# Reordering the first tile's attention, its first row blocks, the next tile's k copies and the last rows of a fused attention and MLP kernel

## The chip, the cores and the metric

One core of a Trainium2 chip. The metric is the device time of one execution in microseconds (us), median of several. Executions of one and the same kernel scatter here by about 2 us, which is as large as the effects looked for. So I read segments of profiles beside times, and give 95% intervals with every ratio.

## The reference

Chunked attention (chunks of 64 tokens, head size 64), then an MLP with exact Gelu:

```python
q, k, v: (8, 8, 576, 64) float32
scores = q_c @ k_c^T / 8;  attn = softmax(scores);  x = attn @ v_c      # per chunk of 64
h = x @ w_in (512 x 2048);  g = 0.5 * h * (1 + erf(h / sqrt(2)));  out = g @ w_out (2048 x 512)
```

The kernel cuts the 4608 tokens into nine tiles of 512. For each tile TensorE makes q k^T, the AV products (x), then `mm1` (h) and `mm2` (y); the attention of the next tile is woven into the present tile's mm2.

## The kernel before

The parts that the change and the argument touch; "..." marks cuts. An "AV" is the group of matmuls that makes x for one head pair; a "spread" is sixteen small matmuls that copy the reciprocals of the softmax sums to where x needs them; a "cast" turns a loaded float32 piece into bfloat16.

```python
DV, AC, PO = nc.vector.tensor_copy, nc.scalar.copy, nc.gpsimd.tensor_copy

def att_Tk(t, g, copy):                       # k of head pair g, transposed into two diagonal halves
    tp = transposed(t, "k", g)                # four 128x128 transposes into one PSUM bank
    for r in range(2):
        sl = slice(CH * r, CH * (r + 1))
        copy(k_bds[g][sl, :, sl].rearrange(...), tp[sl])
...
T += [lambda g=g: att_Tq(t, g, cq), lambda g=g: att_Tk(t, g, ck if t == 0 or g < 2 else DV)]
...
def att_total(t, g0, g1):                     # tiles 2 to 8: the softmax sums, on VectorE
    ...
    nc.vector.tensor_tensor(total[:, g0:g1], part[:, g0:g1], other[:, g0:g1], op=add)
    nc.vector.reciprocal(rb[:, g0:g1], total[:, g0:g1])
...
def mm1_slot(t, f, n=1, between={}):          # n blocks of h at a time, step by step over ks
    ...
    for ks in range(KS):
        for a in range(n):
            nc.tensor.matmul(h_ps[a][:], w_in_sb[:, ks, ...], st["x"][:, ks, :], ...)
    for a in range(n):
        nc.scalar.activation(st["h"][:, f + a, :], h_ps[a][:], Act.Gelu)
...
def last_rows(t, ms):                         # the last 128 rows: two groups of 256 columns
    h = d_model // 2
    for a, (pool, tag) in enumerate(((ps_mm, "mm"), (ps_at, "at"))):
        y_ps = pool.tile([P, h], f32, ...)
        for f in range(FF):
            nc.tensor.matmul(y_ps[:], ...[P rows of h], w_out_sb[:, f, a * h:(a + 1) * h], ...)
        y_sb = ypool.tile([P, h], f32, ...)
        (AC if a == 0 else DV)(y_sb[:], y_ps[:])
        for c in range(P // CH):
            (nc.sync if c == 0 else nc.scalar).dma_start(out[..., a * h:(a + 1) * h], y_sb[...])

def mm2_rows(t, f):                           # tile 0's mm2: block f of w_out for four row blocks
    for ms in range(MT // P):
        if f == 0:
            pool, tag = (ps_at, "at") if ms == 3 else (ps_mm, "mm")
            tiles[t]["y_ps", ms] = pool.tile(...)
        nc.tensor.matmul(tiles[t]["y_ps", ms][:], ..., start=(f == 0), stop=False)
...
A[0](); p2(); A[1](); p3(); A[2](); keep_warm(1); A[3]()     # AVs; p2, p3 spread the sums
win.append(load_w_in(NWC - 1)); wout = [load_w_out(0)]
for i, eng in enumerate((PO, AC, DV, PO)):                   # casts of the first w_in chunk
    win[0](i, eng)
act_table(Act.Gelu)
```

The loads are issued in one order: tile 0's q, k, v, then w_in, then w_out, q, k and v of tile 1 in between.

The softmax here doesn't subtract the row's maximum and nothing guards it: scores larger than these inputs give would overflow.

Of the kernel before, what the change touches and what calls it, by code (L numbers as in the profile page):

```python
# [11 lines left out]
def kernel(  # L12
# [9 lines left out]
    nc = tc.nc  # L22
    P = 128
    f32 = mybir.dt.float32
    bf16 = mybir.dt.bfloat16
    Act = mybir.ActivationFunctionType

    B, H, S, D = q.shape
    CH = 64
    NC = S // CH  # L30
    J = 4
    PC = CH // J
    G = H // 2
    d_model = H * D
# [3 lines left out]
    MT = CT * CH  # L38
    NT = B + 1
    KS = d_model // P  # L40
    FF = d_ff // P
# [27 lines left out]
    k_bds = [consts.tile([P, CT, P], bf16, name=f"k_bd{i}") for i in range(G)]  # L69
# [10 lines left out]
    w_out_sb = consts.tile([P, FF, d_model], bf16, name="w_out_sb")  # L80
# [10 lines left out]
    ypool = ctx.enter_context(tc.tile_pool(name="ypool", bufs=4))  # L91
    ps_mm = ctx.enter_context(tc.tile_pool(name="ps_mm", bufs=3, space=bass.MemoryType.PSUM))
    ps_tp = ctx.enter_context(tc.tile_pool(name="ps_tp", bufs=2, space=bass.MemoryType.PSUM))
    ps_at = ctx.enter_context(tc.tile_pool(name="ps_at", bufs=3, space=bass.MemoryType.PSUM))
# [6 lines left out]
    tiles = [dict() for _ in range(NT)]  # L101
# [38 lines left out]
    def transposed(t, nm, g):  # L140
        pool, tag = (ps_tp, "tp") if t or nm == "q" else (ps_mm, "mm")
        tp = pool.tile([P, 2, J, P], bf16, tag=tag, name="tp")
        for j in range(J):
            nc.tensor.transpose(tp[:, 0, j], tiles[t][nm][:, g, j].rearrange("p r d -> p (r d)"), ident[:])  # L144
        return tp[:, 0].rearrange("p j (i c) -> p i c j", i=CT)

    def att_Tq(t, g, copy):
        tp = transposed(t, "q", g)
        qT = work.tile([P, CT, CH], bf16, tag="qT", name="qT", bufs=5)
        copy(qT[:].rearrange("p i (c j) -> p i c j", j=J), tp)  # L150
        tiles[t]["qT", g] = qT

    def att_Tk(t, g, copy):
        tp = transposed(t, "k", g)
        for r in range(2):
            sl = slice(CH * r, CH * (r + 1))
            copy(k_bds[g][sl, :, sl].rearrange("p i (c j) -> p i c j", j=J), tp[sl])  # L157


    def flip(t, nm):  # L160
# [7 lines left out]
    def flip_k(t, g, copy):  # L168
        src = flipped(t, "k", g)
        for r in range(2):  # L170
            sl = slice(CH * r, CH * (r + 1))
            copy(k_bds[g][sl, :, sl].rearrange("p i (c j) -> p i c j", j=J), src[sl])  # L172

    def att_S_flipped(t, g):

        st = tiles[t]
        s_ps = ps_at.tile([P, CT, CH], f32, tag="at", name="s_ps")
        qt = st["qt"][:, g * J:(g + 1) * J].rearrange("p j (i c) -> p i j c", i=CT)
        for i in range(CT):
            nc.tensor.matmul(s_ps[:, i, :].rearrange("p (j c) -> p j c", j=J), k_bds[g][:, i, :], qt[:, i],  # L180
                             start=True, stop=True)
        pT = work.tile([P, CT, CH], bf16, tag="pT", name="pT", bufs=5)
        nc.scalar.activation(pT[:].rearrange("p i (c j) -> p i c j", j=J),  # L183
                             s_ps[:].rearrange("p i (j c) -> p i c j", j=J), Act.Exp, scale=scale)
        st["pT", g] = pT

    def att_S(t, g):
        st = tiles[t]
        pool, tag = (ps_tp, "tp") if t == 1 and g > 1 else (ps_at, "at")
        s_ps = pool.tile([P, CT, CH], f32, tag=tag, name="s_ps")  # L190
        for i in range(CT):
            nc.tensor.matmul(s_ps[:, i, :], k_bds[g][:, i, :], st["qT", g][:, i], start=True, stop=True)  # L192
        pT = work.tile([P, CT, CH], bf16, tag="pT", name="pT", bufs=5)
        nc.scalar.activation(pT[:], s_ps[:], Act.Exp, scale=scale)  # L194
        st["pT", g] = pT
# [49 lines left out]
    def att_total(t, g0, g1):  # L245

        part, other, total, rb = (tiles[t][nm] for nm in ("part", "other", "total", "rb"))
        for s in range(G):
            o = s ^ 1
            nc.scalar.copy(other[QD * s:QD * (s + 1), g0:g1], part[QD * o:QD * (o + 1), g0:g1])  # L250
        nc.vector.tensor_tensor(total[:, g0:g1], part[:, g0:g1], other[:, g0:g1], op=mybir.AluOpType.add)
        nc.vector.reciprocal(rb[:, g0:g1], total[:, g0:g1])
# [46 lines left out]
    DV, AC, PO = nc.vector.tensor_copy, nc.scalar.copy, nc.gpsimd.tensor_copy  # L299

    def att_units(t, cq=DV, ck=DV):
        tiles[t]["x"] = xpool.tile([P, G, MT], bf16, tag="x", name="x")
        T = []
        for g in range(G):
            T += [lambda g=g: att_Tq(t, g, cq), lambda g=g: att_Tk(t, g, ck if t == 0 or g < 2 else DV)]
        S_ = [lambda g=g: att_S(t, g) for g in range(G)]
        if t > 1:
            T = [lambda g=g: flip_k(t, g, ck) for g in range(G)]
            S_ = [lambda g=g: (att_S_flipped(t, g), att_part(t, g)) for g in range(G)]
        if t > 0:  # L310
            U = [lambda g=g: att_total(t, g, g + 2) for g in (0, 2)] + [lambda g=g: att_rc(t, g) for g in range(G)]
        else:
            U = [lambda g=g: att_sum(t, g) for g in range(G)]
        A = [lambda g=g: att_av(t, g) for g in range(G)]
        return T, S_, U, A
# [46 lines left out]
                nc.sync.dma_start(out[m0:m0 + CH, :], y_sb[c * CH:(c + 1) * CH, :])  # L362

    def last_rows(t, ms):
        h = d_model // 2
        for a, (pool, tag) in enumerate(((ps_mm, "mm"), (ps_at, "at"))):
            y_ps = pool.tile([P, h], f32, tag=tag, name="y_ps")
            for f in range(FF):
                nc.tensor.matmul(y_ps[:], tiles[t]["h"][:, f, ms * P:(ms + 1) * P],  # L369
                                 w_out_sb[:, f, a * h:(a + 1) * h], start=(f == 0), stop=(f == FF - 1))  # L370
            y_sb = ypool.tile([P, h], f32, tag="y", name="y_sb")
            (AC if a == 0 else DV)(y_sb[:], y_ps[:])
            for c in range(P // CH):
                m0 = (ms * (P // CH) + c) * S + MT
                (nc.sync if c == 0 else nc.scalar).dma_start(
                    out[m0:m0 + CH, a * h:(a + 1) * h], y_sb[c * CH:(c + 1) * CH, :])

    def mm2_rows(t, f):

        for ms in range(MT // P):  # L380
            if f == 0:
                pool, tag = (ps_at, "at") if ms == 3 else (ps_mm, "mm")
                tiles[t]["y_ps", ms] = pool.tile([P, d_model], f32, tag=tag, name="y_ps")
            nc.tensor.matmul(tiles[t]["y_ps", ms][:], tiles[t]["h"][:, f, ms * P:(ms + 1) * P], w_out_sb[:, f, :],  # L384
                             start=(f == 0), stop=False)

    def phase(t, extra1, extra2, by_rows=False, between={}):
        nms = MT // P
        order = [(ms, qt) for ms in range(nms) for qt in range(NQ)]
        if by_rows:  # L390
            order = [(None, f) for f in range(FF - FC)] + [(ms, NQ - 1) for ms in range(nms)]
        first = 3 if t == 1 else 1
        mm1_slot(t, 0, first, between)
        for f in range(first, FF):
            for u in extra1.get(f, ()):
                u()
            mm1_slot(t, f)
        for s, (ms, qt) in enumerate(order):
            for u in extra2.get(s, ()):
                u()  # L400
            if ms is None:
                mm2_rows(t, qt)
            else:
                mm2_slot(t, ms, qt)
        for u in extra2.get("end", ()):
            u()
# [33 lines left out]
    def keep_warm(n):  # L440
        warm = ps_mm.tile([P, MT], f32, tag="mm", name="warm")
        for _ in range(n):
            nc.tensor.matmul(warm[:], rest[:, 0:P], rest[:], start=True, stop=True)
# [3 lines left out]
    def act_table(func):  # L447
        nc.scalar.activation(act_scratch[:], rest[:, 0:1], func)  # L448

    with tc.manual_schedule():  # L450
# [4 lines left out]
        win = [load_w_in(c, 2 if c < 2 else 1) for c in range(NWC - 1)]  # L455
# [3 lines left out]
        zero_k(k_bds[1], nc.gpsimd)  # L459
        zero_v(0, nc.vector)  # L460
        T, S_, U, A = att_units(0, DV, AC)
        cast_qk(0, "k", 0, PO)
        zero_k(k_bds[2], nc.gpsimd)
# [30 lines left out]
        p2 = att_sum_pe(0, 2)  # L494
        p3 = att_sum_pe(0, 3)
        A[0]()
        p2()
        A[1]()
        p3()
        A[2]()  # L500
        keep_warm(1)
        A[3]()
        win.append(load_w_in(NWC - 1))
        wout = [load_w_out(0)]
        for i, eng in enumerate((PO, AC, DV, PO)):
            win[0](i, eng)
        act_table(Act.Gelu)
        load_qk(1, "q")
        wout.append(load_w_out(1))
        for c in range(1, NWC):  # L510
# [6 lines left out]
            if c < 3:  # L517
                r = slice(CH * (c - 1), CH * c)
# [19 lines left out]
        T, S_, U, A = att_units(1, AC, AC)  # L538
# [16 lines left out]
        for t in range(1, NT):  # L555
            nxt = t + 1 < NT
            if nxt:
                T, S_, U, A = att_units(t + 1)
# [44 lines left out]
```

## Time and profile before

| | before |
|---|---|
| median time | 290.65 us (290.45 to 291.22, 4 runs) |
| span of the profiled run | 288.9 us |
| TensorE busy | 278.2 us, 96% |
| first AV to first mm2 matmul | 13.99 to 31.72: 17.73 us |
| first mm2 matmul to the k transposes of tile 1 | 31.72 to 39.07: 7.35 us |
| those to the last x of tile 1 | 39.07 to 52.12: 13.05 us |
| last x to the last rows' first matmul | 52.12 to 281.55: 229.43 us |
| tail: from there to the end | 281.55 to 288.9: 7.35 us |

With the 13.99 us ahead of the first AV the five stretches make up the span. The span is given to 0.1 us, so the tail is good to about 0.05. The lines behind the stretches are in the prediction.

### The profile page before, as it was taken

To read this page: it belongs to the slowest core of one execution; us is meant where nothing else is said; L and a number is where in the kernel's file an instruction comes from. 1 tells how busy PE (TensorE), PEld (TensorE's weight loads), DVE (VectorE), ACT (ScalarE), POOL (GpSimd) and SP (SyncE) were. 2 spreads that over 40 slices of the span, in tenths; PEclk is the share of its full clock that TensorE was granted. 3 is DMA by queue.
4 is the path that set the end of the run, shared out by engine and by line. 5 is a ranking of instruction groups with operands and counts; after the bars stand their busy time and mean duration, and the time that the engine had idled before them with its cause. 6 is when DMAs were issued, how large, how long until landed. Compare 5 with 4: busy or idle time off the path is not lost.

```text
span 288.9 us, 4859 instructions
## 1 busy us (share of the span) xinstructions
PE 278.2 (96%) x1836; PEld 138.5 (48%) x1870; DVE 154.8 (54%) x265; ACT 170.1 (59%) x329; POOL 98.8 (34%) x136
## 2 busy tenths in 40 slices
PE   7699999999999999999999999999999999999994
PEld 2454455445544554455445544554455445544444
DVE  6854349348805882749246935394268425850011
ACT  3767766967447844785468536763785368626400
POOL 6859758605651830262008400650003610000000
PEclk9999999999999999999999999999999999999999
DMA  6999999999799726961698259914999970120033
GB/s 222 247 360 404 393 337 265 254 207 286 191 291 311 168 99 161 325 145 74 161 261 234 76 138 285 233 73 115 163 130 131 265 147 2 39 106 2 0 73 73
DMA packets 96887, 53.79 MB, mean 186 GB/s; under 512 B 68576, under 2 KB 89312, under 8 KB 96864
## 3 DMA queue, kind: packets, MB, share of 16 engines
q1 hardware_dynamic: 96704, 53.36, 69.8%
q8 instruction: 14, 0.23, 0.3%
q10 hardware_dynamic: 160, 0.13, 0.2%
q14 instruction: 9, 0.07, 0.1%
HBM read 36.70 MB, written 9.44 MB: 160 GB/s over the span
## 4 chain that ended last, share of the span: by engine, by line
PE 90%; DVE 3%; ACT 3%; DMA 2%; issue 1%; SPq 0%; POOL 0%; DVEq 0%; POOLq 0%
PE h_ps L328 42%; PE y_ps L344 37%; PE av_ps L289 3%; PE y_ps L384 3%; PE s_ps L180 2%; DMA arrival<-in_k_dram 2%; ACT k_bd L157 2%; PE y_ps L369 1%; DVE x L296 1%; PE tp L144 1%; PE rc_ps L276 1%; DVE rc L259 1%; ACT pT L194 1%; SPq L112 0%; PE s_ps L192 0%
## 5 line engine op out<-in xcount | busy, mean ns | idle before, releaser
L328 PE MATMUL h_ps<-x,w_in_sb 128*128 128x512 bf16 x565 | 125.8, 379 | 1.0 <-DVE x L296 0.4
L331 ACT ACTIVATE h<-h_ps 128x512 bf16<-128x512 f32 x144 | 85.5, 597 | 62.5 <-PE h_ps L328 62.4
L344 PE MATMUL y_ps<-w_out_sb,h 128*128 128x512 bf16 x493 | 117.9, 379 | 0.9
L328 PEld LDWEIGHTS <-w_in_sb 128*128 128x128 bf16 x576 | 56.2, 98 | 68.4 <-issue 1.2
L344 PEld LDWEIGHTS <-h 128*128 128x128 bf16 x512 | 46.0, 98 | 46.5 <-issue 0.2
L172 DVE COPY k_bd<-k_t 64x512 bf16<-64x512 bf16 x56 | 35.6, 636 | 53.6 <-DMA k_t<-k_nat 52.6
L133 POOL CAST q_nat<-arrival 128x512 bf16<-128x512 f32 x31 | 21.2, 720 | 95.0 <-DMA arrival<-in_q_dram 95.0
L137 POOL CAST v_bd<-arrival 64x512 bf16<-64x512 f32 (+1 forms) x30 | 36.3, 1210 | 20.5 <-DMA arrival<-in_v_dram 13.3
L296 DVE TENSOR_TENSOR x<-av_ps,rc 128x512 bf16<-128x512 f32 x36 | 24.8, 692 | 4.7 <-PE av_ps L289 1.4
L133 POOL CAST k_nat<-arrival 128x512 bf16<-128x512 f32 x34 | 20.1, 625 | 11.2 <-DMA arrival<-in_k_dram 9.2
L448 ACT ACT_TABLE_LOAD x18 | 23.1, 1283 | 1.0 <-PEq L587 0.7
L353 DVE COPY y_sb<-y_ps 128x512 f32<-128x512 f32 x11 | 7.6, 691 | 29.7 <-PE y_ps L344 27.8
L353 ACT COPY y_sb<-y_ps 128x512 f32<-128x512 f32 x24 | 13.8, 580 | 14.7 <-PE y_ps L344 14.4
L239 DVE STREAM_TRANSPOSE pt<-pT 128x256 f32<-128x256 f32 x28 | 12.2, 437 | 18.8 <-ACT pT L183 18.8
L259 DVE STREAM_TRANSPOSE rc<-rb 128x512 f32<-128x512 f32 x31 | 21.5, 692 | 0.2 <-ACT rb L229 0.2
L242 DVE TENSOR_REDUCE part<-pt 128x16 f32<-128x512 bf16 x28 | 19.2, 686 | 1.0
L250 ACT COPY other<-part 32x32 f32<-32x32 f32 x56 | 12.0, 215 | 10.4 <-DVE part L242 9.9
L289 PEld LDWEIGHTS <-v_bd 128*128 128x128 bf16 x288 | 13.0, 98 | 8.0 <-issue 0.3
L183 ACT ACTIVATE pT<-s_ps 128x512 bf16<-128x512 f32 x28 | 14.7, 590 | 0.0
L289 PE MATMUL av_ps<-pT,v_bd 128*128 128x64 bf16 x288 | 14.3, 193 | 0.2
L180 PEld LDWEIGHTS <-k_bd 128*128 128x128 bf16 x224 | 10.4, 98 | 6.6
L384 PE MATMUL y_ps<-w_out_sb,h 128*128 128x512 bf16 x46 | 11.9, 379 | 0.4 <-ACT h L331 0.3
(68 smaller groups left out, 136.5 us busy)
## 6 DMA issues: line engine op xcount, KB each, us to landing
arrival<-in_v_dram SPq DMA_DIRECT2D x72, 128.0 KB, 4.1
out_dram<-y_sb SPq DMA_DIRECT2D x32, 256.0 KB, 2.3
arrival<-in_q_dram SPq DMA_DIRECT2D x7, 1024.0 KB, 6.7
arrival<-in_k_dram SPq DMA_DIRECT2D x7, 1024.0 KB, 9.1
arrival<-in_moe_w_out_dram SPq DMA_DIRECT2D x4, 1024.0 KB, 12.2
arrival<-in_moe_w_in_dram SPq DMA_DIRECT2D x4, 512.0 KB, 6.2
arrival<-in_moe_w_in_dram SPq DMA_DIRECT2D x2, 1024.0 KB, 10.4
arrival<-in_q_dram SPq DMA_DIRECT2D x4, 256.0 KB, 4.7
```

What stands on the lines that cost most here:

```text
L133: copy(st[nm][:, g].rearrange("p j r d -> p r j d"), st[nm + "f"][:, 2 * g:2 * g + 2])
L137: copy(v_bds[t % NV][sl, :, gs, sl].rearrange("p i g d -> p g i d"), tiles[t]["vf"][sl, gs])
L172: copy(k_bds[g][sl, :, sl].rearrange("p i (c j) -> p i c j", j=J), src[sl])
L259: nc.vector.transpose(rc[:], src.to_broadcast([P, NB, 32]))
L289: nc.tensor.matmul(av_ps[:, i, :], v_bds[t % NV][:, i, g, :], st["pT", g][:, i, :], start=True, stop=True)
L296: nc.vector.tensor_tensor(x, av, rc, op=mybir.AluOpType.mult)
L328: nc.tensor.matmul(h_ps[a][:], w_in_sb[:, ks, (f + a) * P:(f + a + 1) * P], st["x"][:, ks, :], start=(ks == 0), stop=(ks == KS - 1))
L331: nc.scalar.activation(st["h"][:, f + a, :], h_ps[a][:], Act.Gelu)
L344: nc.tensor.matmul(y_ps[:], st["h"][:, f, ms * P:(ms + 1) * P], w_out_sb[:, f, :], start=(f == 0), stop=(f == FF - 1))
L353: (AC if ms < 3 and t + 1 < NT else DV)(y_sb[:], y_ps[:])
L384: nc.tensor.matmul(tiles[t]["y_ps", ms][:], tiles[t]["h"][:, f, ms * P:(ms + 1) * P], w_out_sb[:, f, :], start=(f == 0), stop=False)
L448: nc.scalar.activation(act_scratch[:], rest[:, 0:1], func)
```

## The change

Four parts: (1) tile 0's second AV ahead of the first spread, one warming matmul less, the second w_in cast from ScalarE to VectorE and ahead of the last x, the load of the Gelu table ahead of the other casts, and mm1 of tile 0 begins with two blocks at a time; (2) the first mm2 takes row block 3 first and row block 2's first matmul late; (3) of each k tile ScalarE copies one half, VectorE the other; (4) the last rows are one group of 512 columns, whose halves ScalarE and VectorE copy.

```diff
-    def att_Tk(t, g, copy):
+    def att_Tk(t, g, copies):
...
-            copy(k_bds[g][sl, :, sl]..., tp[sl])
+            copies[r](k_bds[g][sl, :, sl]..., tp[sl])
...
-            ... att_Tk(t, g, ck if t == 0 or g < 2 else DV)]
+            ... att_Tk(t, g, (ck, ck if t == 0 else DV))]
...
     def last_rows(t, ms):
+        y_ps = ps_mm.tile([P, d_model], f32, tag="mm", name="y_ps")
+        for f in range(FF):
+            nc.tensor.matmul(y_ps[:], ..., w_out_sb[:, f, :], start=(f == 0), stop=(f == FF - 1))
+        y_sb = ypool.tile([P, d_model], f32, tag="y", name="y_sb")
         h = d_model // 2
-        (two groups of 256 columns, as above)
+        AC(y_sb[:, 0:h], y_ps[:, 0:h])
+        DV(y_sb[:, h:], y_ps[:, h:])
+        (one transfer of 64 whole rows on each queue)
...
     def mm2_rows(t, f):
-        for ms in range(MT // P):
+        todo = [(f, ms) for ms in (3, 0, 1, 2)]
+        if f < 2:
+            todo = [(f, ms) for ms in (3, 0, 1)] if f == 0 else [(1, 3), (1, 0), (1, 1), (0, 2), (1, 2)]
+        for f, ms in todo:
...
-        first = 3 if t == 1 else 1
+        first = (2, 3, 1)[min(t, 2)]
...
         A[0]()
+        A[1]()
         p2()
-        A[1]()
+        A[2]()
+        win[0](1, DV)
         p3()
-        A[2]()
-        keep_warm(1)
         A[3]()
         win.append(load_w_in(NWC - 1))
         wout = [load_w_out(0)]
-        for i, eng in enumerate((PO, AC, DV, PO)):
+        act_table(Act.Gelu)
+        for i, eng in ((0, PO), (2, DV), (3, PO)):
             win[0](i, eng)
-        act_table(Act.Gelu)
```

More of the change, by code (lines that the diff above doesn't have):

```diff
@@ L156, in att_Tk @@
             sl = slice(CH * r, CH * (r + 1))
-            copy(k_bds[g][sl, :, sl].rearrange("p i (c j) -> p i c j", j=J), tp[sl])
+            copies[r](k_bds[g][sl, :, sl].rearrange("p i (c j) -> p i c j", j=J), tp[sl])
     def flip(t, nm):
@@ L304, in att_units @@
         for g in range(G):
-            T += [lambda g=g: att_Tq(t, g, cq), lambda g=g: att_Tk(t, g, ck if t == 0 or g < 2 else DV)]
+            T += [lambda g=g: att_Tq(t, g, cq), lambda g=g: att_Tk(t, g, (ck, ck if t == 0 else DV))]
         S_ = [lambda g=g: att_S(t, g) for g in range(G)]
@@ L364, in last_rows @@
     def last_rows(t, ms):
-        h = d_model // 2
-        for a, (pool, tag) in enumerate(((ps_mm, "mm"), (ps_at, "at"))):
-            y_ps = pool.tile([P, h], f32, tag=tag, name="y_ps")
-            for f in range(FF):
-                nc.tensor.matmul(y_ps[:], tiles[t]["h"][:, f, ms * P:(ms + 1) * P],
-                                 w_out_sb[:, f, a * h:(a + 1) * h], start=(f == 0), stop=(f == FF - 1))
-            y_sb = ypool.tile([P, h], f32, tag="y", name="y_sb")
-            (AC if a == 0 else DV)(y_sb[:], y_ps[:])
-            for c in range(P // CH):
-                m0 = (ms * (P // CH) + c) * S + MT
-                (nc.sync if c == 0 else nc.scalar).dma_start(
-                    out[m0:m0 + CH, a * h:(a + 1) * h], y_sb[c * CH:(c + 1) * CH, :])
+        y_ps = ps_mm.tile([P, d_model], f32, tag="mm", name="y_ps")
+        for f in range(FF):
+            nc.tensor.matmul(y_ps[:], tiles[t]["h"][:, f, ms * P:(ms + 1) * P], w_out_sb[:, f, :],
+                             start=(f == 0), stop=(f == FF - 1))
+        y_sb = ypool.tile([P, d_model], f32, tag="y", name="y_sb")
+        h = d_model // 2
+        AC(y_sb[:, 0:h], y_ps[:, 0:h])
+        DV(y_sb[:, h:], y_ps[:, h:])
+        for c in range(P // CH):
+            m0 = (ms * (P // CH) + c) * S + MT
+            (nc.sync if c == 0 else nc.scalar).dma_start(out[m0:m0 + CH, :], y_sb[c * CH:(c + 1) * CH, :])
     def mm2_rows(t, f):
-        for ms in range(MT // P):
+        todo = [(f, ms) for ms in (3, 0, 1, 2)]
+        if f < 2:
+            todo = [(f, ms) for ms in (3, 0, 1)] if f == 0 else [(1, 3), (1, 0), (1, 1), (0, 2), (1, 2)]
+        for f, ms in todo:
             if f == 0:
```

## The prediction

> **What bounds the kernel now.** I read the page first, then who waited for whom on TensorE, then the timeline of the places that the diff touches. The page's engine shares:
>
> ```profile
> PE 278.2 (96%) x1836; PEld 138.5 (48%) x1870; DVE 154.8 (54%) x265; ACT 170.1 (59%) x329; POOL 98.8 (34%) x136
> ```
>
> TensorE (PE) is the bound. The question is where its missing 4% lies. The waits of TensorE between 53 us and the end are one line (the same 0.2 us that opens the window):
>
> ```profile
> PE h_ps L328 <- DVE x L296: 0.2, 1, 0.2
> ```
>
> So from 52.87 us on TensorE never waits: whatever the change wins or loses earlier is carried unchanged to the end, and only the last few us (results out of PSUM, to memory) can add to it. All parts of the diff lie before 52.87 us or after 281 us. The three stretches, from the timeline (start, duration, engine, line, tiles, count, idle before it and who ended it):
>
> ```profile
> 17.22 1.29 DVE L296 TENSOR_TENSOR x<-av_ps,rc 128x512 bf16<-128x512 f32 x2 [0.74 <-PE av_ps L289]
> 17.40 0.94 PE L328 MATMUL h_ps<-x,w_in_sb 128*128 128x512 bf16 x3
> 18.56 5.77 PE L328 MATMUL h_ps<-x,w_in_sb 128*128 128x512 bf16 x26 [0.22 <-DVE x L296]
> ...
> 31.72 0.59 PE L384 MATMUL y_ps<-w_out_sb,h 128*128 128x512 bf16 x2
> 32.57 0.59 PE L384 MATMUL y_ps<-w_out_sb,h 128*128 128x512 bf16 x2 [0.25 <-ACT h L331]
> ```
>
> First, the first tile's mm1 does three of the four steps of its first block and stops for the last x (18.52). Second, the first mm2 does two row blocks and stops for a PSUM buffer that the last Gelu still reads. Matmuls of 512 columns go 0.216 us apart (60 of them between 18.56 and about 31.5), so the second stop costs 32.57 - (31.72 + 2 x 0.216) = 0.42 us. Then the next tile's attention inside that mm2:
>
> ```profile
> 39.07 0.61 PE L144 MATMUL tp<-ident,k_nat 128*128 128x128 bf16 x8
> 39.50 2.36 ACT L157 COPY k_bd<-tp 64x512 bf16<-64x512 bf16 x4 [1.96 <-PE tp L144]
> 40.72 0.38 PE L144 MATMUL tp<-ident,k_nat 128*128 128x128 bf16 x4 [0.17 <-ACT k_bd L157]
> 41.14 2.81 DVE L157 COPY k_bd<-tp 64x512 bf16<-64x512 bf16 x4 [2.90 <-PE tp L144]
> 44.01 0.72 DVE L204 STREAM_TRANSPOSE t<-sum_ps 128x512 f32<-128x512 f32 x1
> 45.68 0.81 DVE L432 CAST w_out_sb<-arrival 128x512 bf16<-128x512 f32 x1
> 46.41 0.70 DVE L221 STREAM_TRANSPOSE t<-sums_ps 128x512 f32<-128x512 f32 x1
> 52.12 0.69 DVE L296 TENSOR_TENSOR x<-av_ps,rc 128x512 bf16<-128x512 f32 x1
> ```
>
> From 41.1 to 52.8 us VectorE (DVE) is nearly continuous, and the last x it makes ends the wait at 52.87. So in this stage DVE's chain sets the time, not TensorE. Last, the tail:
>
> ```profile
> 281.55 3.66 PE L369 MATMUL y_ps<-w_out_sb,h 128*128 128x256 bf16 x32
> 283.50 0.37 ACT L372 COPY y_sb<-y_ps 128x256 f32<-128x256 f32 x1 [11.51 <-PE y_ps L369]
> 285.24 0.42 DVE L372 COPY y_sb<-y_ps 128x256 f32<-128x256 f32 x1 [2.75 <-PE y_ps L369]
> ```
>
> The first half's copy hides behind the second half's matmuls; after the last matmul comes one copy of 0.42 us, then a transfer and the closing, 288.9 - 285.66 = 3.24 us.
>
> **What the skill says.** The Trainium skill, "PSUM — Partial Sum Buffer", section "PSUM bank collisions raise a hardware error": no two engines may touch one bank and quadrant at once, two readers included. No trace yet shows this, but it decides two parts: in the listing of the changed program's instructions, the DVE copy of the last rows and each DVE copy of a k half wait for a ScalarE (ACT) semaphore, where the old DVE copies waited for TensorE. Two engines on one bank run **one after the other**. "TensorE: Matmul & The Clock Gate", "Back-to-back issue gap": 262 cycles at 256 columns, 518 at 512, so two halves cost almost what one whole costs; the trace agrees for 512 (0.216 us; the 131 ns that the page also gives for a stream is not seen). "DMA: Bandwidth & Descriptors", "Anatomy of one DMA": about 2.0 us fixed plus bytes over 436 GB/s, given for the software path; the page of before has 2.3 us for 128 KB and 1.9 to 2.2 us for 64 KB on the hardware queues, which fits.
>
> **Part 1, AVs ahead of the spreads, two blocks at a time.** TensorE's work from 13.99 is four AVs, two spreads of 1.02, and one warming matmul of 0.22, which goes. New order: A0 14.0, A1 14.3, spread 14.6 to 15.6, A2 to 15.95, spread to 16.97, A3 to about 17.25. On ACT the second rc copy (0.58) runs 17.08 to 17.66, then DVE's x takes 0.69, to 18.38: the last x comes only 0.14 earlier than 18.52. But the first two blocks of mm1 now share their wait. The second block's weights are now cast on DVE after the third x, by about 17.45, and the six matmuls of the first three steps then run to about 18.58, past the last x. Both blocks are done at 19.01; before it was 18.56 + 5 x 0.216 = 19.64. The third block's weights are cast by DVE after the last x (0.70, to about 19.1), so mm1 goes on at 19.13. **Gain 0.5.** Later weight casts end 0.1 us or more ahead of their new need (the closest: 24.18 for 24.3).
>
> **Part 2, reordered row blocks.** Row block 3 has a free buffer and goes first; five more matmuls (1.08 us) follow before block 2, whose buffer comes free about 0.8 us after mm1's end. The stop of 0.42 is gone. **Gain 0.42, in all 0.92**; step 7 (the k transposes) starts at 38.15 instead of 39.07. The k casts are done by 37.9.
>
> **Part 3, k halves.** As parallel copies they would shorten ACT's 2 x 0.585 to 0.70. As serial copies a half pair takes 0.59 + 0.03 + 0.70, so the third transpose waits until 38.58 + 1.32 + 0.05 = 39.95: 1.80 after step 7's start, where before it was 40.72 - 39.07 = 1.65. The pairs pipeline at DVE's pace, 0.70 each; but the third transposes go out only at 39.95 and the fourth after the next four mm2 matmuls (41.26). I place DVE's four copies at 39.2, 39.9, 41.0 and 42.3, the last done at 43.0 instead of 43.95. The sum's transpose, bound to TensorE's order (sum matmul at 42.8), then starts at 43.23 instead of 44.01. From there the DVE chain is the same instructions, and the last weights (arrived 43.15) and v casts (third head pair done 48.30, wanted 48.5) are just in time. **So 0.78 is left of 0.92** when mm1 of tile 1 resumes, at 52.1.
>
> **Part 4, last rows.** Matmuls: 16 x 0.216 = 3.45 instead of 32 x 0.110 = 3.51, gain 0.06. Copies: 0.37 on ACT, a hop of 0.04, then 0.42 on DVE, all after the last matmul: loss 0.41 against 0.42 alone. Transfer: 2 x 128 KB at the end instead of 2 x 64 KB; by the measured landings 0.1 to 0.4 more, by the page's rate 128 KB / 436 GB/s = 0.30 (estimate); I take 0.25. **Loss 0.60.**
>
> **Sum:** -0.78 + 0.60 = -0.18, so 290.73 - 0.18 = 290.55, say **290.6**.
>
> **Rivals.** (a) The halves do run side by side: tail 0.37 shorter, k chain 0.15 or more better, 290.0. For it: the author's evident aim, and that disjoint columns look independent. Against: the listed wait. (b) The early gain is eaten by arrivals, which don't move: DMA was 99% busy in several slices up to 50 us, GpSimd's v casts run gapless 44.27 to 49.65, and the third w_out chunk is cast only at 39.64. Then only the tail's loss stays: 291.3. Against: each cast stands ahead of its new need by my times, if by only 0.1 to 0.2. (c) DVE's chain after 44 us doesn't start earlier, since it holds four k copies as before: gain 0.3, in all 291.0. Against: its first copy comes at 39.2, not 41.14.
>
> **Range and chances.** The rivals span 290.0 to 291.3, and three runs of before spread 0.8; so 289.9 to 291.3. Two per cent is 5.8 us, and all of the parts together never touch more than about 2 us: within 2% at 0.98, 0.01 on either side.
>
> **What would show it.** Right: no TensorE idle before the last x of tile 0 (part 1) and none between the first mm2 row blocks (part 2); ACT then DVE on each k pair without overlap, the third transpose about 1.8 after step 7's start; mm1 of tile 1 resuming at 52.1; the tail with ACT 0.37 and then DVE 0.42, and 3.5 us from there to the end. Wrong: overlapping copies (rival a), TensorE waiting for a cast at 40 or 46 to 48 us (b), or tile 1 resuming at 52.5 or later (c).

## The result, and the profile after

Median 291.98 us (291.19 to 292.09, 4 runs) against 290.65: ratio 1.0036, interval 1.0014 to 1.0059. A ratio is the mean time of one kernel's fast runs over that of the other's of the same rounds, so it is not quite the ratio of the quoted medians. The profiled run's span went from 288.9 to 290.3 us. So the change is 1.3 us slower where I had said 0.1 faster, outside my range.

The lines after, in the order of those before. Engine shares, from the page of the changed kernel:

```profile
PE 280.8 (97%) x1853; PEld 137.1 (47%) x1853; DVE 155.7 (54%) x266; ACT 169.3 (58%) x328; POOL 98.0 (34%) x136
```

The waits of TensorE after 53 us, changed kernel (in total, times, longest). Before there was none but the one that opens the window; this one lies at 106.7 us:

```profile
PE av_ps L289 <- DVE x L296: 0.4, 1, 0.4
```

Timeline of the changed kernel at tile 0's mm1 and mm2, and at tile 1's k (start, duration, what; in brackets the idle time before it and who ended it):

```profile
16.94 0.61 POOL L427 CAST w_in_sb<-arrival 128x512 bf16<-128x512 f32 x1 [0.60 <-DMA arrival<-in_moe_w_in_dram]
16.96 0.87 DVE L427 CAST w_in_sb<-arrival 128x512 bf16<-128x512 f32 x1
17.60 6.71 PE L328 MATMUL h_ps<-x,w_in_sb 128*128 128x512 bf16 x30 [0.22 <-POOL w_in_sb L427]
24.35 1.18 DVE L427 CAST w_in_sb<-arrival 128x512 bf16<-128x512 f32 x2 [2.08 <-DMA arrival<-in_moe_w_in_dram]
...
31.76 1.89 PE L387 MATMUL y_ps<-w_out_sb,h 128*128 128x512 bf16 x8
38.69 0.61 PE L144 MATMUL tp<-ident,k_nat 128*128 128x128 bf16 x8
39.12 1.06 ACT L157 COPY k_bd<-tp 64x512 bf16<-64x512 bf16 x2 [1.96 <-PE tp L144]
39.73 1.30 DVE L157 COPY k_bd<-tp 64x512 bf16<-64x512 bf16 x2 [0.65 <-ACT k_bd L157]
40.48 0.38 PE L144 MATMUL tp<-ident,k_nat 128*128 128x128 bf16 x4 [0.31 <-DVE k_bd L157]
40.53 2.29 POOL L435 CAST w_out_sb<-arrival 128x512 bf16<-128x512 f32 x4 [0.98 <-DMA arrival<-in_moe_w_out_dram]
41.20 1.02 PE L387 MATMUL y_ps<-w_out_sb,h 128*128 128x512 bf16 x4
44.03 0.72 DVE L204 STREAM_TRANSPOSE t<-sum_ps 128x512 f32<-128x512 f32 x1 [0.24 <-PE sum_ps L200]
52.10 0.69 DVE L296 TENSOR_TENSOR x<-av_ps,rc 128x512 bf16<-128x512 f32 x1
```

The stops on the last x of tile 0 and on the last Gelu are gone, as foreseen. But GpSimd's first w_in cast now starts when the load lands, 16.94 (before, it started at 16.34 as soon as GpSimd was free), and mm1 waits for it. Beside it VectorE's cast of the second block took 0.87 us, where in tail_undone (below) it ran alone and took 0.42. Further on the third w_in piece landed for 24.35 (before, 23.75); its first cast, of 0.43 us, ended at 24.78, and mm1's next matmul, due at about 24.59, went at 24.84. The third w_out chunk lands for 40.53 (before 39.64), and mm2 waits for that cast until 41.20. By the last x, 52.10 against 52.12, nothing of the early gain is left. The tail:

```profile
282.06 3.62 PE L368 MATMUL y_ps<-w_out_sb,h 128*128 128x512 bf16 x16
285.71 0.37 ACT L372 COPY y_sb<-y_ps 128x256 f32<-128x256 f32 x1 [13.22 <-PE y_ps L368]
286.12 0.43 DVE L373 COPY y_sb<-y_ps 128x256 f32<-128x256 f32 x1 [3.11 <-ACT y_sb L372]
286.57 0.47 SPq L376 DMA_DIRECT2D out_dram<-y_sb  x1
```

VectorE's idle time is ended by ScalarE: the copies go one after the other. The account of the 1.40 us of span:

| stretch | predicted | measured (before, after) |
|---|---|---|
| up to the first AV | 0 | +0.05 (13.99, 14.04) |
| first AV to first mm2 matmul | -0.50 | -0.01 (17.73, 17.72) |
| to the k transposes of tile 1 | -0.42 | -0.42 (7.35, 6.93) |
| to the last x of tile 1 | +0.14 | +0.36 (13.05, 13.41) |
| to the last rows | 0 | +0.53 (229.43, 229.96) |
| tail | +0.60 | +0.89 (7.35, 8.24) |

### The profile page after: what moved, and what is told of

It is laid out like the page before. It is cut to its first block, busy times and chain, and to the rows that moved or that the text cites. A ratio compares the mean times of both kernels' runs of the same rounds, so it can differ in the third digit from the quotient of the medians.

```text
span 290.3 us, 4853 instructions
## 1 busy us (share of the span) xinstructions
PE 280.8 (97%) x1853; PEld 137.1 (47%) x1853; DVE 155.7 (54%) x266; ACT 169.3 (58%) x328; POOL 98.0 (34%) x136
## 4 chain that ended last, share of the span: by engine, by line
PE 80%; DMA 10%; DVE 4%; ACT 2%; SPq 1%; POOL 1%; issue 0%; DVEq 0%
PE h_ps L328 38%; PE y_ps L344 34%; DMA arrival<-in_moe_w_out_dram 8%; PE av_ps L289 3%; DMA arrival<-in_k_dram 2%; PE s_ps L180 2%; PE y_ps L387 1%; PE y_ps L368 1%; SPq L112 1%; DVE total L251 1%; DVE part L242 1%; DVE x L296 1%; DVE pt L239 1%; ACT L451 0%; POOL v_bd L137 0%
## 5 line engine op out<-in xcount | busy, mean ns | idle before, releaser
L344 PE MATMUL y_ps<-w_out_sb,h 128*128 128x512 bf16 x512 | 120.5, 379 | 0.0
L172 DVE COPY k_bd<-k_t 64x512 bf16<-64x512 bf16 x56 | 34.9, 623 | 55.9 <-DMA k_t<-k_nat 54.9
L133 POOL CAST q_nat<-arrival 128x512 bf16<-128x512 f32 x31 | 20.3, 691 | 95.1 <-DMA arrival<-in_q_dram 92.8
L387 PE MATMUL y_ps<-w_out_sb,h 128*128 128x512 bf16 x48 | 11.8, 379 | 0.1
```

Of the source, the lines that this page charges most:

```text
L133: copy(st[nm][:, g].rearrange("p j r d -> p r j d"), st[nm + "f"][:, 2 * g:2 * g + 2])
L172: copy(k_bds[g][sl, :, sl].rearrange("p i (c j) -> p i c j", j=J), src[sl])
L344: nc.tensor.matmul(y_ps[:], st["h"][:, f, ms * P:(ms + 1) * P], w_out_sb[:, f, :], start=(f == 0), stop=(f == FF - 1))
```

## The experiments

Eighteen runs. My theory A: what parts 1 and 2 save is eaten, at least in part, by weights that land late, by chance; what is left is lost at the tail, and in a later wait for VectorE (theory B). The segments of all profiles under the kernel's own loads, from their timelines (us; "w_in" is the start of GpSimd's first w_in cast). The first AV, ahead of every edit, lies anywhere from 13.65 to 14.89, so read w_in against it: in the change mm1 can begin 3.18 us after the first AV (tail_undone) and the cast takes 0.61, so by my estimate w_in delays it when its cast starts more than some 2.5 us after the first AV:

| profile | first AV | w_in | AV to mm2 | to k | to last x | to last rows | tail | span |
|---|---|---|---|---|---|---|---|---|
| before | 13.99 | 16.34 | 17.73 | 7.35 | 13.05 | 229.43 | 7.35 | 288.9 |
| before_again | 13.86 | 16.27 | 17.73 | 7.35 | 13.01 | 229.43 | 7.32 | 288.7 |
| before_look3 | 14.48 | 17.71 | 18.72 | 7.35 | 13.02 | 229.42 | 7.31 | 290.3 |
| tail_only | 13.65 | 16.21 | 17.73 | 7.35 | 13.01 | 229.42 | 8.14 | 289.3 |
| tail_two_banks | 14.14 | 16.64 | 17.75 | 7.35 | 13.01 | 229.43 | 7.82 | 289.5 |
| split_before | 14.33 | 18.33 | 18.49 | 7.35 | 13.01 | 230.10 | 7.32 | 290.6 |
| rows_only | 14.28 | 17.33 | 17.73 | 6.94 | 13.01 | 229.43 | 7.31 | 288.7 |
| rows_only_2 | 14.12 | 16.48 | 17.72 | 6.94 | 13.03 | 229.42 | 7.27 | 288.5 |
| after (the change) | 14.04 | 16.94 | 17.72 | 6.93 | 13.41 | 229.96 | 8.24 | 290.3 |
| after_again | 14.88 | 17.25 | 17.39 | 7.30 | 13.71 | 230.32 | 8.20 | 291.8 |
| tail_undone | 14.06 | 16.25 | 17.08 | 6.94 | 13.44 | 229.42 | 7.56 | 288.5 |
| tail_undone_2 | 14.49 | 16.87 | 17.27 | 7.06 | 13.72 | 230.51 | 7.55 | 290.6 |
| split_tail | 14.89 | 17.30 | 17.60 | 6.94 | 13.15 | 230.11 | 7.51 | 290.2 |
| start_rows | 14.45 | 17.65 | 17.88 | 6.94 | 13.15 | 230.15 | 7.53 | 290.1 |
| start_only | 13.88 | 16.65 | 17.45 | 7.35 | 13.00 | 229.77 | 7.55 | 289.0 |

### Unaltered kernels again: after_again, before_again, before_look3

No edit.

> The changed kernel, unaltered, for a second profile. Theory A (arrivals): the first pieces of w_in land at a time that varies from run to run and not with the change; here the first w_in cast of GpSimd starts anywhere from 16.3 to 17.0 us, and wherever it starts, the last weights' casts (about 40 and 44 us) follow with the same shift and mm1 of tile 1 resumes within 0.3 us of 52.8. Rival (the change itself delays the loads): the w_in cast starts at 16.9 again, and the w_out cast at 40.5 again. Time 1.003 to 1.005 of before either way. If the 0.4 us wait of tile 2's last AV (106.7 us) is chance, it is gone or of another size in this profile.

> The kernel before, unaltered, for a second profile on this chip. Theory A: its w_in arrival varies too (16.3 to 17.0), with mm1 of tile 1 resuming at 52.5 to 53.5. Rival: arrivals again as in the first profile (16.3; w_out cast at 39.6).

> A third look at the kernel before. If lateness is chance for both starts, the first AV or the first w_in cast may be late here too (first AV after 14.3 or w_in after 16.5). If it belongs to the changed start: 13.6 to 14.2 and 16.2 to 16.6 again.

Measured: after_again 292.78 us (291.29 to 293.55), ratio 1.0049, interval 1.0017 to 1.0080, and its profile starts late: first AV at 14.88. So w_in at 17.25 is in time (2.37 after the first AV; before, 2.35), and mm1 begins without a stop; but TensorE waited for the third w_in piece and for w_out chunks two and three, and the last x came at 53.28 (not within 0.3 of 52.8, as I had it). The wait at 106.7, of the last AV of tile 3 (the expectation says tile 2, in whose mm2 it stands), is gone, but one like it appeared at 167.3. before_again is as before, 290.42. before_look3, run later, is the telling one: 292.06 us, and in its timeline

```profile
17.71 0.61 POOL L424 CAST w_in_sb<-arrival 128x512 bf16<-128x512 f32 x1 [0.91 <-DMA arrival<-in_moe_w_in_dram]
18.38 3.64 PE L328 MATMUL h_ps<-x,w_in_sb 128*128 128x512 bf16 x16 [0.33 <-POOL w_in_sb L424]
```

So late loads strike the kernel before too, with nothing changed in it: w_in is cast from 16.27 to 17.71 in three looks at the same program, 2.35 to 3.23 after the first AV. Lateness does not need the change. Whether it strikes the change more often, so few profiles cannot tell.

### The tail: tail_undone, tail_only, tail_two_banks

tail_undone (and tail_undone_2) is the change without part 4; tail_only is the kernel before with part 4; tail_two_banks is the kernel before with

```diff
+        y_ps = [pool.tile([P, h], f32, tag=tag, name="y_ps") for pool, tag in ((ps_mm, "mm"), (ps_at, "at"))]
+        for f in range(FF):
+            for a in range(2):
+                nc.tensor.matmul(y_ps[a][:], ..., w_out_sb[:, f, a * h:(a + 1) * h], ...)
+        y_sb = ypool.tile([P, d_model], f32, tag="y", name="y_sb")
+        AC(y_sb[:, 0:h], y_ps[0][:])
+        DV(y_sb[:, h:], y_ps[1][:])
+        (transfers as in the change)
```

> The changed kernel with the old two half groups of last rows. My theory: the tail (from the start of the last rows' matmuls to the end of the span) goes from 8.24 back to 7.35 us, so 0.9 us less than the changed kernel, ratio to before about 1.000 to 1.002. Rival (tail is innocent, loss lies in the middle): time like the changed kernel, 1.0036.

> The kernel before with only the new last rows. My theory: 0.9 us slower than before, ratio 1.003; ACT 0.37, then DVE 0.43 after the last matmul without overlap, then about 3.7 us to the end. If the copies could overlap or the transfer were the same size, 0.0 to 0.4.

> The kernel before with last rows as two interleaved groups of 256 columns in two PSUM banks, then one copy on each engine, and the changed kernel's two transfers of 128 KB. Theory (one bank makes the copies go one after the other): here both copies run at the same time, within 0.1 us of one another, and the tail is about 0.35 us shorter than in tail_only (8.14), so 7.8, of which 0.4 over the old tail is the larger transfer. Rival (the copies wait for something else, such as the shared output tile): still one after the other.

Measured: tail_only 291.83 us, ratio 1.0031 (1.0005 to 1.0056), 0.9 us over before as expected, tail 8.14. tail_undone 291.38, ratio 1.0013 (0.9979 to 1.0046), tail 7.56. Timeline of tail_two_banks:

```profile
285.26 0.37 ACT L372 COPY y_sb<-y_ps 128x256 f32<-128x256 f32 x1 [13.15 <-PE y_ps L369]
285.37 0.42 DVE L373 COPY y_sb<-y_ps 128x256 f32<-128x256 f32 x1 [2.75 <-PE y_ps L369]
```

The output tile is shared as in the change, only the PSUM banks (and with them the tiles) differ, and the copies overlap; the tail is 7.82 where I had expected 7.8. So the shared output tile is not what kept them apart, and a tile of its own in a second bank frees VectorE's copy; bank and tile are not told apart. This fits the Trainium skill, "PSUM — Partial Sum Buffer", "PSUM bank collisions raise a hardware error": there the order is a duty of the program, and the built program carries it as a wait (VectorE's idle time in the change was ended by ScalarE); no run here lets two engines meet in one bank. The rest is the transfer. From the end of the copies to the end of the span it is 3.24 us before, 3.66 in tail_only and 3.71 in tail_two_banks. The landings, from the DMA view of before and of the change (issuing queue, count, KB each, us from issue to landing):

```profile
out_dram<-y_sb SPq DMA_DIRECT2D x1, 64.0 KB, 1.9
out_dram<-y_sb ACTq DMA_DIRECT2D x1, 64.0 KB, 2.2
```

```profile
out_dram<-y_sb SPq DMA_DIRECT2D x1, 128.0 KB, 2.3
out_dram<-y_sb ACTq DMA_DIRECT2D x1, 128.0 KB, 2.6
```

The later one sets the end, and it grew by 0.4. Time did not follow the profile in tail_two_banks: 292.43 us, ratio 1.0046 (1.0018 to 1.0074), slower than tail_only's ratio though its tail is shorter. The profiled run was the fastest of its six; with a scatter of 1.8 us I take the tail from the profiles.

A second look at the change without part 4:

> A second look at the changed kernel with the old last rows. If chance: first AV near 14.0 and w_in by 16.5 about as often as in the kernel before. If it belongs to the changed start: first AV at 14.8 or w_in cast after 16.9, as in three or four of its six relatives.

292.36 us, first AV 14.49, w_in 16.87: a late start, in the job where before_look3 was late as well, though w_in is in time after its first AV (2.38). Neither branch of the expectation is clearly met. Here w_out came late twice and 1.09 us was lost after the last x. The first look shows what the change saves when w_in is there in time. Timeline of tail_undone:

```profile
16.25 0.61 POOL L427 CAST w_in_sb<-arrival 128x512 bf16<-128x512 f32 x1
17.24 14.06 PE L328 MATMUL h_ps<-x,w_in_sb 128*128 128x512 bf16 x64
38.08 0.61 PE L144 MATMUL tp<-ident,k_nat 128*128 128x128 bf16 x8
39.95 2.29 POOL L435 CAST w_out_sb<-arrival 128x512 bf16<-128x512 f32 x4 [1.00 <-DMA arrival<-in_moe_w_out_dram]
```

GpSimd goes straight from v to w_in (no idle bracket), mm1 runs 64 matmuls without a stop that the view shows, and first AV to mm2 is 17.08, 0.65 less than before; then part 2's 0.41 follows. Of these 1.06 us, w_out's arrival takes 0.30 back (13.44 to the last x, against 13.14 where w_out is no matter, see below).

### Fewer loads: before_light, after_light, before_early, after_early, kold_early

Their outputs are wrong, which doesn't matter for the times. "light": chunks 1 to 3 of w_out are cast from chunk 0's buffer. "early": besides, tile 0's v is cast from q's buffer and not loaded. after_light and after_early have the old last rows; kold_early also has the old k copies.

```diff
-        raw = stage_tile()[:].rearrange("p (f n) -> p f n", f=FC)
-        nc.sync.dma_start(raw, w_out_v[:, c * FC:(c + 1) * FC, :])
+        if c == 0:
+            wout_raw.append(stage_tile()[:].rearrange("p (f n) -> p f n", f=FC))
+            nc.sync.dma_start(wout_raw[0], w_out_v[:, c * FC:(c + 1) * FC, :])
+        raw = wout_raw[0]
     def load_v(t, gs=range(G)):
+        if t == 0:                                   # "early" only
+            tiles[t]["vf"] = tiles[t]["qs"][:].rearrange("p (g i d) -> p g i d", g=G, d=D)
+            return
```

> The kernel before, but chunks 1 to 3 of w_out are cast from chunk 0's staging buffer, so 3 MB fewer are loaded in the first 45 us; the result is wrong on purpose, every instruction on the engines stays. It is the partner of the next run. Both theories: the same as before or up to 0.5 us less, as before hardly waits for w_out; last x of tile 1 starts at 51.5 to 52.1.

> The changed kernel with the old last rows and the same 3 MB fewer loads (wrong on purpose). Theory A (the early gain was eaten by weights that land at a fixed time): now no TensorE wait for a w_out cast, the k transposes of tile 1 about 0.7 to 0.9 us earlier than in the light kernel before and the last x of tile 1 0.6 to 0.8 us earlier; time 0.5 to 0.8 us under the light kernel before, with less scatter. Rival (DVE's chain after 44 us holds the time whatever arrives): k transposes earlier, but last x of tile 1 within 0.2 us of the light kernel before.

> The kernel before with 4 MB fewer loads in the first 45 us (tile 0's v is cast from q's staging buffer, chunks 1 to 3 of w_out from chunk 0's; wrong on purpose), so that w_in lands well before it is wanted. Partner of the next two. Theory A: first w_in cast of GpSimd no longer ended by an arrival; the TensorE stops on the last x (18.5 us) and on the last Gelu (0.25) stay; last x of tile 1 at 51 to 52.

> The changed kernel with the old last rows and the same 4 MB fewer loads (wrong on purpose). Theory A (arrivals eat the early gain): with no arrival in the way, part 1 and 2 give the 0.9 us that I worked out by the k transposes of tile 1 and 0.5 to 0.8 at the last x of tile 1, and the time is 0.4 to 0.8 us under the partner's. Rival C (the parts are worth less than worked out, whatever arrives): 0.3 us or less.

> As after_early, but with the k copies as before (two tiles on ScalarE, two on VectorE): parts 1 and 2 alone. By my sum the k halves on two engines cost 0.15 us at the third transpose (1.80 against 1.65 after the first) but let VectorE's chain start 0.3 us sooner; so the last x of tile 1 stands 0.2 to 0.4 us later here than in after_early, the time 0.1 to 0.4 us longer. Rival: part 3 is worth nothing, equal within 0.1.

The times miss theory A: before_light 290.70 us (0.9993, 0.9975 to 1.0011), after_light 290.98 (1.0011, 0.9989 to 1.0033); before_early 291.40 (1.0010), after_early 291.83 (1.0024), kold_early 291.71 (1.0021). No gain of 0.4 to 0.8 us appeared. In the light pair the profiles say why: the first AV, ahead of every edit, came at 13.45 in one and 14.11 in the other, and w_in, which I had not made any lighter, was cast at 15.48 and 17.00. Even so the change's k transposes came level, at 38.51 against 38.53. Counted from the first AV they came 0.68 earlier and the last x 0.54 earlier, though mm1 waited for w_in until 17.94: a little under what theory A asked of the profile. In the early kernels I put another wait in place of the one removed: GpSimd now casts without a gap, and VectorE's casts beside it stretch. In kold_early VectorE's second w_in cast took 2.16 us instead of 0.42, and TensorE waited for it until 20.08. So the early runs cannot judge part 1, and the times leave theory A unproved as a whole.

They do measure part 3 cleanly, as no w_out is waited for. From the k transposes to the last x: 13.00 in before_light, before_early and kold_early, 13.14 in after_light and after_early. **The k halves cost 0.14 us**, as my sum had it. My expectation for kold_early (later by 0.2 to 0.4) had the sign wrong.

### The v casts in pieces: split_tail, split_before

```diff
-                for r in range(2):
-                    cast_v(t + 1, r, PO)
+                for g in range(G):
+                    for r in range(2):
+                        cast_v(t + 1, r, PO, slice(g, g + 1))
```

Why: around the lost time near 106 us (tile 3's attention, in tile 2's mm2) the timelines read, before and then changed:

```profile
99.68 3.84 POOL L137 CAST v_bd<-arrival 64x2048 bf16<-64x2048 f32 x2 [1.10 <-DMA arrival<-in_v_dram]
101.36 0.25 DVE L251 TENSOR_TENSOR total<-part,other 128x32 f32<-128x32 f32 x1
102.40 1.16 DVE L251 TENSOR_TENSOR total<-part,other 128x32 f32<-128x32 f32 x1 [0.40 <-ACT other L250]
```

```profile
101.05 3.84 POOL L137 CAST v_bd<-arrival 64x2048 bf16<-64x2048 f32 x2 [0.80 <-DMA arrival<-in_v_dram]
101.34 1.63 DVE L251 TENSOR_TENSOR total<-part,other 128x32 f32<-128x32 f32 x1
103.28 1.65 DVE L251 TENSOR_TENSOR total<-part,other 128x32 f32<-128x32 f32 x1
106.73 0.39 PE L289 MATMUL av_ps<-pT,v_bd 128*128 128x64 bf16 x8 [0.36 <-DVE x L296]
```

The small addition takes 0.13 to 0.19 us where nothing is in its way. Here the first ends at 102.97, which is when GpSimd's first cast ends (101.05 + 1.92), the second at 104.93, when the second cast ends. The Trainium skill, "SBUF — State Buffer", "Who interferes with whom", says that a VectorE instruction with two SBUF inputs contends with a GpSimd instruction that reads SBUF, and that the loser is blocked for the whole instruction; this trace agrees. Before, the second of the two additions met a cast and the first only a cast's end; in the change the casts began 1.4 us later and both did, and VectorE's chain of x ran out of slack.

> The changed kernel with the old last rows, and the v casts of tiles 2 to 8 on GpSimd in eight pieces instead of two. Theory B (DVE's small total operation stands still until GpSimd's running cast of 1.9 us ends, and that makes the later wait of TensorE): no total operation over 0.8 us, no TensorE wait after 53 us in the profile, time 0.2 to 0.6 us less than the unsplit kernel on the average (290.5 to 291.0), less scatter. Rival (the scatter is all from the first 53 us): time as the unsplit one, 291.3.

> The kernel before with the same split of the v casts, as a control. Theory B: total operations no longer over 0.8 us; time 0 to 0.3 us less than before, since before TensorE seldom waits there; its slowest runs (292) get rarer. Rival: no change at all.

Measured: no addition over 0.62 us in either profile, and no wait near 106 or 166 us, so the mechanism is right (the additions are the stronger sign, as tail_undone, unsplit, has no such wait either). The time is not: split_tail 291.87 us, 1.0035 (1.0009 to 1.0061), split_before 291.26, 1.0017 (0.9994 to 1.0041). The pieces brought a new wait, in both kernels; from the timeline of split_tail:

```profile
69.15 0.41 PE L180 MATMUL s_ps<-q_t,k_bd 128*128 128x64 bf16 x8 [0.51 <-DVE k_bd L172]
```

VectorE's k copies, between SBUF and SBUF, now met the pieces: the eight ahead of this wait took 6.83 us, and 4.96 in before. That is 0.67 us from the last x to the last rows in both.

### The parts alone: rows_only, rows_only_2, start_rows, start_only

rows_only is the kernel before with the new `mm2_rows` alone, start_only has part 1 alone, start_rows parts 1 and 2.

> The kernel before with the reordered row blocks (part 2) alone. From the profiles: the stretch from the first mm2 matmul to the k transposes of tile 1 goes from 7.35 to 6.94 us, and from there to the last x of tile 1 stays 13.0 unless w_out lands after 40.3. Theory A: 0.3 to 0.4 us less than before, ratio 0.9986 to 0.999, since the old start feels w_in's arrival little. Rival (any early gain is eaten by w_out's arrival): 0.1 or less.

> Parts 1 and 2 without the k halves and without the new last rows. Where w_in has landed by 16.3 us: first AV to first mm2 matmul 17.1 instead of 17.73, k transposes 0.4 after that gain again, last x 13.0 after the k transposes unless w_out is late; then 1.0 us under before. Where w_in is late: 17.4 to 17.7 and no gain of part 1. Theory A: on the mean of the runs 0.2 to 0.6 us under before with a wider scatter. Rival (the changed start itself delays the loads): 0.2 us or more over before, as tail_undone was.

> Reordered row blocks alone, again. Theory A: first mm2 matmul to k transposes 6.94 us again, last x 13.0 after them, no wait after 53 us, and 0.3 to 0.5 us under before, ratio near 0.9985. Rival (the first ratio was luck of the arrivals): within 0.1 us of before.

> Part 1 alone (AVs ahead of the spreads, two blocks at a time, the second w_in cast on VectorE). Theory A: first AV to first mm2 matmul 17.1 us with w_in in time, 17.4 to 17.9 with w_in late, against 17.73 (18.5 to 18.7 when late) before; part of it is given back by late w_out or by a wait near 106 or 166 us. Time within 0.3 us of before. Rival (part 1 is a loss by itself): 0.4 us or more over before.

Measured: rows_only 290.44 us against 291.17, ratio 0.9982 (0.9951 to 1.0013); again 290.38 against 291.17, 0.9981 (0.9956 to 1.0007). Both profiles show 6.94 from mm2 to the k transposes, 13.0 after that, and no wait after 53 us. start_rows 291.07, 0.9995 (0.9969 to 1.0020). start_only 291.41, 1.0025 (0.9998 to 1.0051), with w_in at 16.65 and 17.45 from first AV to mm2, 0.34 us lost after the last x (the same pair of blocked additions, 1.10 and 1.65, at 160 us). TensorE waits there for w_in too: its first weight load, at 17.31, for GpSimd's cast, the next, at 17.60, for the cast that part 1 moved to VectorE, which took 0.74 us beside GpSimd's.

I had overlooked one more line, here from start_only's VectorE:

```profile
164.37 0.69 DVE L296 TENSOR_TENSOR x<-av_ps,rc 128x512 bf16<-128x512 f32 x1 [0.46 <-DVE rc L259]
```

VectorE stands idle for 0.46 to 0.48 us before the first x of tile 5 in all ten profiles with part 1 (light and early ones too), and in none of the ten without. before_early has the same two long additions at tile 5 (1.09 and 1.65) without this idle time, and loses nothing; start_only loses 0.34. What VectorE waits for there the profile does not show.

So part 2 keeps its 0.41 in the profiles, part 1 does not show its gain in time, and the best version by its mean is rows_only: by the ratio 0.5 us under before in both jobs, though each interval still includes 1.

## Why the prediction was wrong

**Right in mechanism and size:** part 2 (-0.42; 6.93 or 6.94 in six of the eight full-load profiles that have it; in the other two, after_again and tail_undone_2, the second w_out chunk was late, cast at 36.53 and 35.78 against 34.8 after), part 3 (0.14; the third transposes 1.79 after step 7's start, predicted 1.80), and ScalarE's and VectorE's copies of one bank in turn (0.37, then 0.43). One reason given was wrong: the skill's rule is for one bank and quadrant, a quadrant being 32 partitions, and the k halves lie on partitions 0 to 63 and 64 to 127. So the rule does not decide part 3; the wait in the built program does (VectorE's k copy idle until ScalarE's ends, 0.65).

**The step that failed first:** "Later weight casts end 0.1 us or more ahead of their new need." I took the arrivals of one profile as fixed times. They move: the first w_in cast started 2.2 to 4.0 us after the first AV in the profiles of full loads (16.2 to 18.3 us), and the change needs it by some 2.5 (estimate from tail_undone: mm1 can begin at 3.18, the cast takes 0.61). In the profile after, the pieces of w_in came 0.6 later, and mm1 stopped twice: 0.38 at its start, and 0.25 at the third piece, the one that I had named the closest (24.18 for 24.3; it was ready at 24.78 for 24.59). So -0.50 became -0.01. At the third w_out chunk the same gave another +0.22 over my 0.14. Where w_in was in time (tail_undone) part 1 was worth 0.65. My rival (b) named this, and I set it aside with margins of 0.1 to 0.2 us.

**The second:** "So from 52.87 us on TensorE never waits: whatever the change wins or loses earlier is carried unchanged to the end." VectorE's chain before each mm1 has little slack, and where both additions meet GpSimd's v casts, TensorE can wait: +0.53 in the profile after. Both being long is not enough: with 0.70 and 1.60 (tail_undone) or 0.96 and 1.65 (before_light) nothing was lost. None of the seven full-load profiles with the old start and whole v casts shows it, five of the six with part 1 do. No order of instructions differs there, and in the light and early runs it does not appear with part 1 either. Four of the five lie at tile 5, where part 1 brings VectorE's idle time of 0.46 to 0.48 as well; the one in the profile after lies at tile 3, where there is no such idle time. What makes that idle time, and what puts the v casts later against VectorE, is open.

**A term mis-sized:** the last transfer, 0.25, measured 0.42 (tail_only) to 0.51 (the change). With the 0.37 of the serial copy, part 4 costs 0.79 to 0.89 and not 0.60. tail_only's time (1.0031) bears it out.

**Open:** part 1 alone is 0.7 us slower on the mean, with an interval that just reaches 1; its one profile, of the fastest of its six runs, explains some 0.3 of it (-0.28, +0.34, and a tail of 7.55 where the old start has 7.3). That tail is 7.51 to 7.56 in all full-load kernels with part 1 and the old last rows; the profiles show a longer closing wait on TensorE's sequencer (0.9 against 0.6 us in start_only and rows_only_2), and I don't know why. No run shows either that the change makes its loads late or that it does not.

## What to carry to other kernels

Ask of each wait that you remove what the next one is, and how fixed its time is: a load's landing time from one profile is one draw, and a margin of 0.1 us against it is none. To split one PSUM bank's eviction between two engines gave here the sum of the two copies, not the larger; use two banks, or leave the first half's copy hidden behind the second half's matmuls. At the end of this kernel 64 KB more on each queue after the last matmul cost 0.42 to 0.51 us, so a half that can leave early is worth its own group.

## What the Trainium skill lacked or had wrong

- "PSUM — Partial Sum Buffer": it has the collision, but not the price of a shared bank. Here two copies of 256 columns from one bank took 0.37 + 0.43 us in turn; from two banks they started 0.11 us apart.
- "TensorE: Matmul & The Clock Gate", "Back-to-back issue gap": a sustained 131 ns for 512 columns is not seen; in the steady stretches matmuls go 216 ns apart, which the page calls the isolated gap there (an earlier part of the same page has about 216 ns back to back).
- "DMA: Bandwidth & Descriptors", "Anatomy of one DMA": 2.0 us plus bytes over 436 GB/s, given for the software path, gave 0.30 us for 128 KB more at the end (estimate); the end moved by 0.42 to 0.51. Also, the same 128 KB landed 2.3 us after issue on SyncE's queue and 2.6 on ScalarE's (64 KB: 1.9 and 2.2); no page has that.
- No page says how far landing times scatter: with the same loads in the same order the first piece of w_in was cast from 16.2 to 18.3 us, 2.2 to 4.0 after the first AV.
